# A recurrent attention layer with a gated feed-forward layer on one core: the order of every engine taken from a task graph with a list schedule, and deeper rings for the feed-forward weights

## The chip, the cores and the metric

The kernel runs on one core of a Trainium2 chip. TensorE (PE) multiplies matrices, VectorE (DVE) and ScalarE (ACT) do the element-wise work and copy results out of PSUM, GpSimd (POOL) does a few small things, and SyncE (SP) issues nearly all DMAs. Each engine works through its own queue in order; semaphores make one wait for another. The metric is the device time of one execution in microseconds. Before the change the median of three runs is 2511.51 us (2511.01 to 2513.72).

## What is computed

Two layers stand one behind the other, and the pair is applied twice. The first, A, is attention with a recurrent memory: the 2048 rows are cut into 64 segments of 32, and the output of a segment's first 8 rows is the memory of the next segment, so that the 64 segments must run one after the other. The second, B, is a gated feed-forward layer on each row.

```python
mem = mem0                                   # 8 rows of 512
for s in range(64):
    h = concat([mem, x[s*32:(s+1)*32]])      # 40 rows of 512
    q, k, v = h @ Wq, h @ Wk, h @ Wv         # 32 heads of 128
    p = softmax(mask(q @ k.T * scale))       # 40 x 40 in each head
    o = (p @ v) @ Wo                         # 40 rows of 512
    mem = o[:8]; out[s] = o[8:]
# B: out = (sigmoid(x @ w_gate) * (x @ w_up)) @ w_down, with 1792 hidden columns
x = x + A(layernorm(x));  x = x + B(layernorm(x))
x = x + A(layernorm(x));  x = x + B(layernorm(x))   # the same weights again
```

## The kernel before, in words

**Jobs and steps.** The two applications of A are two jobs, j = 0 and j = 1. Job 1 runs six segments behind job 0 (`LAG`), and one step works on one segment of each, so that the matmuls have 80 columns instead of 40. There are 70 steps: six with job 0 alone, 58 with both, six with job 1 alone. Blocks of four segments make 128 rows; layer B works on such a block ("an FFN block"): 16 blocks for each job, 32 in all.

**One step** (`emit_step`). The input of the step stands transposed in a slot of `hT`. For units of three heads PE computes q and k (L239) into one of three PSUM banks `pj`, ACT copies them to `qku`, PE multiplies them to scores in the bank `s_ps` (L255). Six heads make a group; for each group DVE adds the mask (L263), takes the maximum (L266), subtracts it (L267), ACT takes the exponential (L270), DVE sums (L272), inverts (L273) and multiplies (L277, once for each job) into `pb`. PE transposes `pb` into `pt_ps` (L289), and DVE copies it to `ptsb` (L99). Behind all groups come the values v (L325, `pj` again), the product p v (L336, bank `ot_ps`), its copy by ACT, and the product with Wo (L312, bank `wo_ps`, summed over all heads). At the end DVE copies the memory rows into the next slot of `hT` (L358): with that the next step can begin.

**One FFN block** (`task_post`). Behind the fourth step of a block PE transposes the attention output (L438), DVE adds the residual, a layernorm follows (DVE, one POOL instruction, ACT, a transpose on PE, L392), then seven pairs of hidden columns: 16 matmuls for gate and up (L460), a tanh on ACT, one DVE instruction that frees the bank, and last seven pieces of two matmuls with w_down (L496). All of this shares one PSUM bank, `misc`. The weights of B are loaded anew for each block, in pieces of 256 KB: `wg` and `wu` in rings of two, `wd` in a ring of two:

```python
self.gpool = ctx.enter_context(tc.tile_pool(name="gp", bufs=2))   # wg, wu
self.dpool = ctx.enter_context(tc.tile_pool(name="dp", bufs=2))   # wd
```

**What sets the order.** The code is written step by step; the FFN block of job 0 is emitted at once behind the fourth step, that of job 1 in four portions over four steps (`run`, `task_post`). The tile framework's scheduler then orders each engine's instructions by priorities that follow the order of emission; it may pull instructions ahead where a buffer is free.

Of the kernel before, what the change touches and what calls it, by code (L numbers as in the profile page):

```python
# [1 line left out]

# [19 lines left out]
LWP = LW  # L22
BLK = 4
EPS = 1e-5
PRIO_STEP = 1000000
# [5 lines left out]

class Kern:
    def __init__(self, ctx, tc, x_in, mem0, Wq, Wk, Wv, Wo, w_gate, w_up, w_down, out,
                 lag=6, ring=8, groups=None, npj=3, log=None):
        self.ctx, self.tc = ctx, tc
        self.nc = nc = tc.nc
        self.log = log
# [11 lines left out]
        self.LAG = lag  # L49
        self.R = ring  # L50
        assert ring > lag
        self.NSTEPS = self.NSEG + lag
        self.scale = float(DH) ** -0.5
        if groups is None:
            n6 = H // 6
            while n6 > 0 and (H - 6 * n6) % 4 != 0:
                n6 -= 1
            assert (H - 6 * n6) % 4 == 0
            sizes = [6] * n6 + [4] * ((H - 6 * n6) // 4)
            groups = []  # L60
            h = 0
            for sz in sizes:
                groups.append((h, sz))
                h += sz
            assert h == H
        self.groups = groups
        self.HG = max(sz for _, sz in groups)
        assert self.HG <= 6
# [4 lines left out]
        self.w_gate, self.w_up, self.w_down = w_gate, w_up, w_down  # L73
        self.npj = npj
        self.pj_i = 0
        self.ev_i = 0
        self.step_no = 0
        self.prio_idx = 0
        self._setup()

    def mark(self, tag, inst, g=-1):
        if self.log is not None:
            self.log.append((self.step_no, g, tag, inst.ins.name))
        return inst

    def set_prio(self, step, sub=0):
        base = int(max(step, 0) * PRIO_STEP + sub * (PRIO_STEP // 2))
        self.prio_idx += 1
        self.tc.cur_priority = base + self.prio_idx

    def evac(self, out, in_, prefer=None):
        nc = self.nc
        eng = prefer
        if eng is None:
            eng = "act" if (self.ev_i % 2 == 0) else "dve"
            self.ev_i += 1
        if eng == "act":
            return nc.scalar.copy(out=out, in_=in_)  # L98
        return nc.vector.tensor_copy(out=out, in_=in_)  # L99

    def next_pj(self):
        t_ = self.pj[self.pj_i % len(self.pj)]
        self.pj_i += 1
        return t_

    def _setup(self):
        self._setup_pools()
        self._load_first()
        self._setup_weights()

    def _load_first(self):
        self.load_mem0()
        for b in range(self.NBLK):
            if BLK * b - 4 < 0:
                self.pre1(b)

    def _setup_weights(self):
        nc = self.nc
        DC = self.DC
        wq_v = self.Wq.rearrange("(c p) h e -> p c (h e)", p=P)  # L120
        wk_v = self.Wk.rearrange("(c p) h e -> p c (h e)", p=P)
        wv_v = self.Wv.rearrange("(c p) h e -> p c (h e)", p=P)
        wo_v = self.Wo.rearrange("h e d -> e h d")
        loads = []
        for (h0, gsz) in self.groups:
            cs = slice(h0 * P, (h0 + gsz) * P)
            loads.append((self.wq[:, :, cs], wq_v[:, :, cs]))
            loads.append((self.wk[:, :, cs], wk_v[:, :, cs]))
        for (h0, gsz) in self.groups:
            cs = slice(h0 * P, (h0 + gsz) * P)  # L130
            loads.append((self.wv[:, :, cs], wv_v[:, :, cs]))
            loads.append((self.wo[:, h0:h0 + gsz, :], wo_v[:, h0:h0 + gsz, :]))
        for i, (dst, src) in enumerate(loads):
            nc.sync.dma_start(out=dst, in_=src)

    def _setup_pools(self):
# [3 lines left out]
        wpool = ctx.enter_context(tc.tile_pool(name="w", bufs=1))  # L140
        cpool = ctx.enter_context(tc.tile_pool(name="c", bufs=1))
        self.cpool = cpool
        self.wq = wpool.tile([P, DC, HE], BF16, name="wq_sb")
        self.wk = wpool.tile([P, DC, HE], BF16, name="wk_sb")
        self.wv = wpool.tile([P, DC, HE], BF16, name="wv_sb")
        self.wo = wpool.tile([P, H, D], BF16, name="wo_sb")
        self.ident = cpool.tile([P, P], BF16, name="ident")
# [5 lines left out]
        self.maskb = cpool.tile([P, L], F32, name="maskb")  # L153
# [4 lines left out]
        nc.sync.dma_start(out=self.maskb[JOFF:LW, :], in_=self.maskb[0:L, :])  # L158
        self.hT = cpool.tile([P, R, DC, LWP], BF16, name="hT_all")
        nc.vector.memset(self.hT[:], 0.0)  # L160
        self.qku = [cpool.tile([P, 3, 4, P], BF16, name=f"qku{i}") for i in range(3)]
        for t_ in self.qku:
            nc.gpsimd.memset(t_[:], 0.0)
        self.qku_i = 0
        self.vsb = [cpool.tile([P, HG * P], BF16, name=f"vsb{i}") for i in range(2)]
        for t_ in self.vsb:
            nc.gpsimd.memset(t_[:], 0.0)
# [26 lines left out]
    def emit_step(self, t):  # L194
# [64 lines left out]
        def emit_softmax(g, gsz):  # L259
# [25 lines left out]
            for hl in range(gsz):  # L285
                o_ap = pt_all[:, hl, cb:cb + ncol]
                if both:
                    o_ap = o_ap.rearrange("p (a b) -> p a b", a=2)
# [313 lines left out]
```

## Time and profile before

| what | before |
|---|---|
| timed runs | 2511.51 us median (2511.01 to 2513.72) |
| profiled execution, span | 2509.0 us |
| PE busy | 2186.8 us (87%) |
| DVE busy | 1322.3 us (53%) |
| ACT busy | 1217.0 us (49%) |
| read from HBM | 195.04 MB, 79 GB/s over the span |

The profile is of one execution, whose span lies 2.5 us below the median of the timed runs. PE's busy time is of matmuls whose ends are modelled and which overlap, so how much of the span PE really has nothing to start is read from the distance between the starts of matmuls, not from this share. A line in the timeline has the start, the time from the first start to the last end, the engine, the line of the kernel, what is written and read, and the count; in brackets is the idle time before it and what ended it.

### The profile page before, as it was taken

The numbers are of one execution on the slowest core, as the hardware profiler recorded it, in microseconds if no ns is written. First come the engines' busy times: TensorE is split into PE (matmuls) and PEld (weight loads), VectorE is DVE, ScalarE is ACT, GpSimd is POOL, SyncE is SP. The second block draws the span as 40 slices with busy tenths as digits, with TensorE's granted clock in tenths as the row PEclk, the third lists the DMA queues.
The fourth block names the chain that finished last, engine by engine and source line by source line (L and its number), as shares of the span: only waits on it lengthen the run. The fifth ranks groups of instructions, "written<-read, shape, count | busy, mean of one in ns | idle before, by whom it ended". The sixth has DMA issues, their size and how long they took to land.

```text
span 2509.0 us, 95297 instructions
## 1 busy us (share of the span) xinstructions
PE 2186.8 (87%) x42676; PEld 1839.6 (73%) x42676; DVE 1322.3 (53%) x3949; ACT 1217.0 (49%) x2829; POOL 52.2 (2%) x94
## 2 busy tenths in 40 slices
PE   5989898989888888898888889888888889988896
PEld 4877777777777777777777777777777777777673
DVE  4545555555555456455545655554564555455452
ACT  3545454545544454454545445454444545454452
POOL 1000000000000000000000000000000000000000
PEclk8999999999999999999999999999999999999997
DMA  9030204132231413213141421314132131413223
GB/s 303 5 91 10 85 19 134 50 108 60 63 94 47 134 35 112 71 48 106 50 134 34 121 63 56 97 51 134 34 111 71 44 107 50 130 35 102 81 62 97
DMA packets 314716, 203.28 MB, mean 81 GB/s; under 512 B 11706, under 2 KB 313794, under 8 KB 314306
## 3 DMA queue, kind: packets, MB, share of 16 engines
q1 hardware_dynamic: 313538, 195.10, 26.6%
q8 instruction: 333, 5.46, 0.9%
q0 software_dynamic: 768, 2.10, 0.2%
q14 instruction: 77, 0.63, 0.1%
HBM read 195.04 MB, written 2.10 MB: 79 GB/s over the span
## 4 chain that ended last, share of the span: by engine, by line
PE 35%; DVE 32%; DMA 19%; ACT 8%; issue 5%; POOL 1%; SPq 0%; ACTq 0%; POOLq 0%; DVEq 0%
PE wo_ps L312 8%; PE misc_ps L460 5%; DVE pb_98 L277 3%; DVE pb_97 L277 3%; PE pj_120 L325 3%; PE pj_121 L325 3%; PE misc_ps L496 3%; PE pj_122 L325 3%; DVE sm_104 L272 2%; PE pt_ps L289 2%; DVE mx_102 L266 2%; PE ot_ps L336 2%; DVE mx_101 L266 2%; DVE st_95 L263 2%; DVE st_96 L263 2%
## 5 line engine op out<-in xcount | busy, mean ns | idle before, releaser
L239 PEld LDWEIGHTS <-wk_sb 128*128 128x128 bf16 x8960 | 468.8, 99 | 9.6 <-issue 2.6
L239 PEld LDWEIGHTS <-wq_sb 128*128 128x128 bf16 x8960 | 457.2, 99 | 15.5 <-issue 8.6
L325 PEld LDWEIGHTS <-hT_all 128*104 128x104 bf16 x2800 | 316.6, 128 | 82.6 <-issue 1.2
L312 PEld LDWEIGHTS <-wo_sb 128*128 128x128 bf16 x8960 | 340.6, 99 | 20.2 <-issue 3.3
L239 PE MATMUL pj_121<-hT_all,wk_sb 128*128 128x80 bf16 (+1 forms) x2992 | 224.3, 198 | 2.5 <-issue 2.5
L239 PE MATMUL pj_122<-hT_all,wk_sb 128*128 128x80 bf16 (+1 forms) x2984 | 224.7, 199 | 0.0
L239 PE MATMUL pj_120<-hT_all,wk_sb 128*128 128x80 bf16 (+1 forms) x2984 | 223.8, 198 | 0.0
L239 PE MATMUL pj_122<-hT_all,wq_sb 128*128 128x80 bf16 (+1 forms) x2984 | 219.3, 198 | 2.0 <-DVE hT_all L363 1.3
L239 PE MATMUL pj_120<-hT_all,wq_sb 128*128 128x80 bf16 (+1 forms) x2984 | 218.8, 198 | 1.6 <-DVE hT_all L363 0.6
L239 PE MATMUL pj_121<-hT_all,wq_sb 128*128 128x80 bf16 (+1 forms) x2992 | 218.8, 198 | 1.7 <-DVE hT_all L358 0.6
L325 PE MATMUL pj_120<-wv_sb,hT_all 128*104 128x384 bf16 (+1 forms) x936 | 217.5, 342 | 0.0
L325 PE MATMUL pj_122<-wv_sb,hT_all 128*104 128x384 bf16 (+1 forms) x932 | 215.7, 341 | 0.0
L325 PE MATMUL pj_121<-wv_sb,hT_all 128*104 128x384 bf16 (+1 forms) x932 | 215.4, 342 | 0.0
L358 DVE CAST hT_all<-wo_ps 128x64 bf16<-128x64 f32 x57 | 12.8, 224 | 364.2 <-PE wo_ps L312 364.2
L312 PE MATMUL wo_ps<-otsb_113,wo_sb 128*128 128x80 bf16 (+1 forms) x4480 | 200.5, 198 | 1.4 <-ACT otsb_113 L98 1.4
L312 PE MATMUL wo_ps<-otsb_114,wo_sb 128*128 128x80 bf16 (+1 forms) x4480 | 187.0, 198 | 1.7 <-ACT otsb_114 L98 1.4
L263 DVE TENSOR_TENSOR st_95<-s_ps,maskb 104x240 f32<-104x240 f32 (+5 forms) x210 | 77.5, 369 | 179.1 <-PE s_ps L255 177.0
L277 DVE TENSOR_TENSOR pb_98<-st_96,rs_106 64x240 bf16<-64x240 f32 (+3 forms) x384 | 142.7, 372 | 4.7
L277 DVE TENSOR_TENSOR pb_97<-st_95,rs_105 64x240 bf16<-64x240 f32 (+3 forms) x384 | 142.5, 371 | 4.2
L270 ACT ACTIVATE st_95<-st_95 104x240 f32<-104x240 f32 (+5 forms) x210 | 79.7, 380 | 90.1 <-DVE st_95 L267 89.5
L98 ACT CAST otsb_114<-ot_ps 128x480 bf16<-128x480 f32 (+3 forms) x210 | 101.9, 485 | 31.6 <-PE ot_ps L336 31.3
L289 PE MATMUL pt_ps<-ident,pb_98 128*128 128x80 bf16 (+1 forms) x1120 | 74.3, 201 | 42.4 <-DVE pb_98 L277 41.5
(2396 smaller groups left out, 3996.9 us busy)
## 6 DMA issues: line engine op xcount, KB each, us to landing
wq_sb<-in_A_Wq_dram SPq DMA_DIRECT2D x4, 768.0 KB, 7.6
wk_sb<-in_A_Wk_dram SPq DMA_DIRECT2D x4, 768.0 KB, 9.5
wv_sb<-in_A_Wv_dram SPq DMA_DIRECT2D x4, 768.0 KB, 11.6
wo_sb<-in_A_Wo_dram SPq DMA_DIRECT2D x4, 768.0 KB, 10.9
wq_sb<-in_A_Wq_dram SPq DMA_DIRECT2D x2, 512.0 KB, 11.4
wk_sb<-in_A_Wk_dram SPq DMA_DIRECT2D x2, 512.0 KB, 11.6
wv_sb<-in_A_Wv_dram SPq DMA_DIRECT2D x2, 512.0 KB, 10.1
wo_sb<-in_A_Wo_dram SPq DMA_DIRECT2D x2, 512.0 KB, 9.0
```

The source lines that it names most:

```text
L98: return nc.scalar.copy(out=out, in_=in_)
L239: self.mark("qk_mm", nc.tensor.matmul(o_ap, lhsT=W[:, c, h * P:(h + 1) * P], rhs=mv(c), start=(c == 0), stop=(c == DC - 1)), g)
L263: self.mark("sm_mask", nc.vector.tensor_tensor(out=st[pr, hs], in0=s_all[pr, hs], in1=self.maskb[pr, :].unsqueeze(1).to_broadcast([npart, ...
L266: self.mark("sm_max", nc.vector.tensor_reduce(out=mx[pr, hs], in_=st[pr, hs], axis=AX.X, op=ALU.max), g)
L270: self.mark("sm_exp", nc.scalar.activation(out=st[pr, hs], in_=st[pr, hs], func=ACTF.Exp, scale=self.scale), g)
L272: self.mark("sm_sum", nc.vector.tensor_reduce(out=sm[pr, hs], in_=st[pr, hs], axis=AX.X, op=ALU.add), g)
L277: self.mark("sm_mul", nc.vector.tensor_tensor(out=pb[pj_, hs, JOFF * j:JOFF * j + L], in0=st[pj_, hs], in1=rs[pj_, hs].unsqueeze(2).to_bro ...
L289: self.mark("t_mm", nc.tensor.matmul(o_ap, lhsT=pb[:, hl, :], rhs=idn, start=True, stop=True), g)
L312: self.mark("wo_mm", nc.tensor.matmul(wo_ps[:, c * ncol:(c + 1) * ncol], lhsT=self.wo[:, h, c * P:(c + 1) * P], rhs=otsb[:, hl, 0:ncol], s ...
L325: self.mark("v_mm", nc.tensor.matmul(pv[0:LWP, 0:vun * P], lhsT=hT[:, c, :], rhs=self.wv[:, c, col0:col0 + vun * P], start=(c == 0), stop= ...
L460: nc.tensor.matmul(gu[:, 2 * i + k, :], lhsT=W[:, c, i * P:(i + 1) * P], rhs=xnT[:, c, :], start=(c == 0), stop=(c == DC - 1))
L496: nc.tensor.matmul(po, lhsT=hT[:, i, :], rhs=wd[:, k, :], start=(i == 0), stop=(i == FC - 1))
```

## The change

The attention's and the feed-forward layer's arithmetic stays as it is. What changes:

- **A task graph.** Each piece of work (one unit's 24 matmuls, one copy, one DVE instruction, one DMA) becomes a `Task` with an engine, an estimated duration and the keys of what it reads and writes. `Planner.plan` runs a list schedule over all tasks when the program is built: at each moment the engine that is free earliest takes, of its ready tasks, the one with the longest remaining chain (`tail`). The tasks are then emitted in the order of their planned starts, under `manual_schedule`, which keeps that order on each engine.
- **FFN pieces as tasks of their own**: half a pair (8 matmuls) and each w_down piece (2 matmuls) can stand anywhere between attention tasks. The order among users of the bank `misc` stays that of the code.
- **Rings**: `wg`, `wu` and `wd` of three buffers each instead of two; `hff` and `xnT` of one instead of two; `ptsb` of three instead of one for each group; `vsb` holds all heads.
- **Groups**: five groups of six heads and one of two (before: four of six, two of four); values in eight units of four heads (before: eight of three and two of four).
- **Engines**: the copies out of `pt_ps` and of the layernorm's transposes may go to ACT or DVE, as planned; the output DMA goes to SP's queue (before: POOL's). The last block no longer uses the `pj` banks.

```diff
+class Planner:
+    LAT = {"PE": 215.0, "DVE": 130.0, "ACT": 140.0, "POOL": 450.0, "SP": 2200.0}
...
+    def plan(self):
+        T = self.tasks
...
+        for tk in reversed(T):
+            m = 0.0
+            for s in tk.succ:
+                same = T[s].eng == tk.eng
+                m = max(m, T[s].tail + (0.0 if same else tk.lat))
+            tk.tail = m + tk.dur + tk.boost
...
+            while q and q[0][0] <= t:
+                _, i = heapq.heappop(q)
+                if T[i].on is None:
+                    heapq.heappush(h, (-T[i].tail, i))
...
+            tk = T[heapq.heappop(h)[1]]
+            tk.on, tk.start = e, t
+            free[e] = t + tk.dur
...
+        order.sort(key=lambda k: (k.start, k.idx))
+        return order
...
-        self.gpool = ctx.enter_context(tc.tile_pool(name="gp", bufs=2))
-        self.dpool = ctx.enter_context(tc.tile_pool(name="dp", bufs=2))
+        self.NG, self.ND = 3, 3
+        self.wg = [c.tile([P, DC, 2 * P], BF16, name=f"wg{i}") for i in range(self.NG)]
+        self.wu = [c.tile([P, DC, 2 * P], BF16, name=f"wu{i}") for i in range(self.NG)]
+        self.wd = [c.tile([P, 2, D], BF16, name=f"wd{i}") for i in range(self.ND)]
...
+            pl.add("SP", 870, lambda wg=wg, fs=fs: nc.sync.dma_start(out=wg[:], in_=self.wgv[:, :, fs]), w=[("wg", gi)])
...
+                pl.add("PE", 2 * DC * mm_ns(P), mm, r=[("xnT", ti), ("wg", gi), ("wu", gi)], w=["misc"])
...
+            pl.add("PE", 2 * mm_ns(512), dm, r=[("hff", hi, ip), ("wd", di)], w=["misc"])
...
+        order = self.pl.plan()
+        with self.tc.manual_schedule():
+            for tk in order:
+                got = tk.fn()
+                if isinstance(got, tuple):
+                    dst, src = got
+                    if tk.on == "ACT":
+                        nc.scalar.copy(out=dst, in_=src)
+                    else:
+                        nc.vector.tensor_copy(out=dst, in_=src)
```

Three places show what that does to the queues. The first is SP's queue around the w_down pieces of one FFN block (`wd`; `wg` and `wu` are gate and up pieces). Before, block 8 of job 0, its first two `wd` having been issued 26 rows earlier:

```order
L453 DMA wg_8_6_26555<-in_B_w_gate_dram 128x4x256
L454 DMA wu_8_6_26556<-in_B_w_up_dram 128x4x256
L453 DMA wg_6_5_27283<-in_B_w_gate_dram 128x4x256
L454 DMA wu_6_5_27284<-in_B_w_up_dram 128x4x256
L453 DMA wg_6_6_27306<-in_B_w_gate_dram 128x4x256
L454 DMA wu_6_6_27307<-in_B_w_up_dram 128x4x256
L493 DMA wd_8_2_26586<-in_B_w_down_dram 128x2x512
L493 DMA wd_8_3_26590<-in_B_w_down_dram 128x2x512
L493 DMA wd_8_4_26594<-in_B_w_down_dram 128x2x512
L493 DMA wd_8_5_26598<-in_B_w_down_dram 128x2x512
L493 DMA wd_8_6_26602<-in_B_w_down_dram 128x2x512
```

And now, at a w_down phase in the middle of the program (the number behind a name is the buffer's):

```order
L528 DMA wg_113<-in_B_w_gate_dram 128x4x256
L529 DMA wu_116<-in_B_w_up_dram 128x4x256
L528 DMA wg_111<-in_B_w_gate_dram 128x4x256
L529 DMA wu_114<-in_B_w_up_dram 128x4x256
L528 DMA wg_112<-in_B_w_gate_dram 128x4x256
L529 DMA wu_115<-in_B_w_up_dram 128x4x256
L551 DMA wd_118<-in_B_w_down_dram 128x2x512
L551 DMA wd_119<-in_B_w_down_dram 128x2x512
L551 DMA wd_117<-in_B_w_down_dram 128x2x512
L551 DMA wd_118<-in_B_w_down_dram 128x2x512
```

Two pieces can be on their way before, three now, and three gate and up pairs of the next block are now asked for ahead of the w_down pieces.

The second place is PE's queue just behind the first q and k unit of a step (`pj`: q, k or v of one unit; `hT`: the step's input). Before, an FFN pair follows and then the next q and k unit, and no v stands near:

```order
L239 LDWEIGHTS wk_sb
L239 MATMUL pj_121<-hT_all,wk_sb 128x80
L460 LDWEIGHTS wg_6_6_27306
L460 MATMUL misc_ps<-xnT_6_25621,wg_6_6_27306 128x128
...
L239 LDWEIGHTS wq_sb
L239 MATMUL pj_122<-hT_all,wq_sb 128x80
```

Now a unit of v, a w_down piece and another unit of v stand between the first unit of q and k and the second:

```order
L385 LDWEIGHTS wk_sb
L385 MATMUL pj_126<-hT_69,wk_sb 128x80
L451 LDWEIGHTS hT_69
L451 MATMUL pj_128<-wv_sb,hT_69 104x512
...
L556 LDWEIGHTS hff_108
L556 MATMUL misc_ps<-wd_119,hff_108 128x512
...
L451 LDWEIGHTS hT_69
L451 MATMUL pj_126<-wv_sb,hT_69 104x512
```

The values moved from the end of the step to its first half, between the units of q and k.

The third place is PE's queue at the seam between two steps. Before (the last Wo product, and what follows in the step at 1309 us of the profile), an FFN pair stands there:

```order
L312 LDWEIGHTS wo_sb
L312 MATMUL wo_ps<-otsb_114,wo_sb 128x80
L460 LDWEIGHTS wg_6_5_27283
L460 MATMUL misc_ps<-xnT_6_25621,wg_6_5_27283 128x128
...
L239 LDWEIGHTS wq_sb
L239 MATMUL pj_121<-hT_all,wq_sb 128x80
```

Now, at one of the seams, the next step's first unit follows at once (at others a w_down piece stands between):

```order
L535 LDWEIGHTS wu_115
L535 MATMUL misc_ps<-xnT_107,wu_115 128x128
L477 LDWEIGHTS wo_sb
L477 MATMUL wo_ps<-otsb_91,wo_sb 128x80
...
L385 LDWEIGHTS wq_sb
L385 MATMUL pj_127<-hT_70,wq_sb 128x80
```

The FFN pair moved to a place just ahead of the last Wo products, where PE would wait for their input.

More of the change, by code (lines that the diff above doesn't have):

```diff
@@ L139, in _setup_pools @@
         HE = H * P
[L140 to L147, printed above, removed]
+        c = ctx.enter_context(tc.tile_pool(name="c", bufs=1))
@@ new lines, in setup_tiles @@
+        self.wq = c.tile([P, DC, HE], BF16, name="wq_sb")
+        self.wk = c.tile([P, DC, HE], BF16, name="wk_sb")
+        self.wv = c.tile([P, DC, HE], BF16, name="wv_sb")
+        self.wo = c.tile([P, H, D], BF16, name="wo_sb")
+        self.ident = c.tile([P, P], BF16, name="ident")
+        self.maskb = c.tile([P, L], F32, name="maskb")
+        self.negh = c.tile([P, 1], F32, name="negh")
+        self.hT = [c.tile([P, DC, LW], BF16, name=f"hT{i}") for i in range(R)]
+        self.qku = [c.tile([P, 3, 4, P], BF16, name=f"qku{i}") for i in range(3)]
```

815 lines of the change are left out of this document (404 added, 411 removed).

## The prediction, made before the change was run

> **What bounds the kernel now.** The page comes first: PE is the busiest engine, yet the chain that ended last runs only to a third over PE.
>
> ```profile
> span 2509.0 us, 95297 instructions
> ...
> PE 35%; DVE 32%; DMA 19%; ACT 8%; issue 5%; POOL 1%; SPq 0%; ACTq 0%; POOLq 0%; DVEq 0%
> ```
>
> PE, DVE and DMAs take turns at holding up the work. How long a step is, the copy of the memory rows shows, which ends each two-job step but the last:
>
> ```profile
> L358 DVE CAST hT_all<-wo_ps x57: 223/224/225, 213.4 to 2253.5; 128x64 bf16<-128x64 f32 x57
> ...
>   PE wo_ps L312: 364.2, 57
> ```
>
> 56 distances in 2040.1 us are 36.43 us a step; and DVE stood idle 364.2/57 = 6.4 us before each copy, while PE did v, p v and Wo. Four neighbouring steps (length, then busy time and count on PE, PEld, DVE, ACT, POOL) are not alike:
>
> ```profile
> 1193.53:1226.64 33.11, 29.90 (x570) 24.62 (x569) 17.23 (x50) 15.87 (x36) 0.58 (x1) 1.00 0.20 62
> 1226.64:1259.46 32.82, 29.47 (x596) 25.41 (x594) 18.77 (x56) 17.56 (x40) 0.56 (x1) 1.00 0.12 35
> 1259.46:1309.00 49.54, 41.65 (x746) 34.64 (x744) 25.62 (x77) 22.32 (x50) 1.71 (x3) 1.00 0.51 148
> 1309.00:1339.48 30.48, 28.54 (x585) 24.79 (x583) 17.11 (x51) 16.60 (x38) 0.00 (x0) 1.00 0.13 37
> ```
>
> The third holds the whole FFN block of job 0 and takes 49.5 us. PE's timeline there gives the pace of each kind of matmul, by the distance of starts:
>
> ```profile
> 1272.44 0.39 PE L460 MATMUL misc_ps<-xnT_8_26398,wg_8_0_26417 128*128 128x128 bf16 x4
> 1272.66 0.39 PE L460 MATMUL misc_ps<-xnT_8_26398,wu_8_0_26418 128*128 128x128 bf16 x4
> ...
> 1273.33 0.38 PE L289 MATMUL pt_ps<-ident,pb_97 128*128 128x80 bf16 x6
> 1273.54 0.26 PE L255 MATMUL s_ps<-qku_86 128*128 128x40 bf16 x4
> 1273.65 0.30 PE L239 MATMUL pj_120<-hT_all,wq_sb 128*128 128x80 bf16 x4
> 1273.79 0.31 PE L239 MATMUL pj_120<-hT_all,wk_sb 128*128 128x80 bf16 x4
> ...
> 1289.57 0.59 PE L496 MATMUL misc_ps<-wd_8_0_26578,hff_8_26416 128*128 128x512 bf16 x2
> 1290.00 0.59 PE L496 MATMUL misc_ps<-wd_8_1_26582,hff_8_26416 128*128 128x512 bf16 x2
> ...
> 1301.84 1.04 PE L325 MATMUL pj_122<-wv_sb,hT_all 128*104 128x512 bf16 x4
> 1302.72 0.38 PE L336 MATMUL ot_ps<-ptsb_110,vsb_92 128*128 128x80 bf16 x6
> 1302.93 1.03 PE L312 MATMUL wo_ps<-otsb_113,wo_sb 128*128 128x80 bf16 x24
> 1303.80 0.82 PE L325 MATMUL pj_120<-wv_sb,hT_all 128*104 128x512 bf16 x3
> ```
>
> So four q or k matmuls take 0.14 us, four scores 0.11, six transposes or p v 0.21, four v of 512 columns 0.88, 24 of Wo 0.87, four gate or up matmuls 0.22, a w_down piece 0.43. By the program a two-job step has 256 q and k (9.1), 64 scores (1.7), 32 transposes and 32 p v (1.1 each), 32 v (7.0) and 128 Wo (4.6): 24.6 us. An FFN block has 112 gate and up matmuls (6.2), seven w_down pieces (3.0) and two or three transposes of 0.22: 9.8 us. Four steps with two blocks need 118.2 us of PE; they took 33.11 + 32.82 + 49.54 + 30.48 = 145.95. PE had nothing to start for 27.8 us, 7 a step. Two kinds of waits make that up:
>
> ```profile
>   DVE pb_98 L277: 41.5, 125
> ...
> 1264.45 0.40 PE L460 MATMUL misc_ps<-xnT_6_25621,wg_6_4_26369 128*128 128x128 bf16 x4 [1.36 <-DMA wg_6_4_26369<-in_B_w_gate_dram]
> ...
> 1293.91 0.59 PE L496 MATMUL misc_ps<-wd_8_2_26586,hff_8_26416 128*128 128x512 bf16 x2 [0.81 <-DMA wd_8_2_26586<-in_B_w_down_dram]
> ```
>
> PE waits for softmax at the transposes (41.5 us in all for one of the two `pb` buffers), and for FFN weights, whose next piece is asked for only when one of two buffers is free. The step at 1309 has two FFN pairs (24.6 + 1.8 = 26.4 us of PE) and still took 30.48: 4.1 us is what attention alone leaves idle; the rest, some 11 of the 27.8, is the FFN's.
>
> **FFN weights.** A piece lands 2.76 us after its issue where it is nearly alone, 4.70 where several are under way:
>
> ```profile
> 1200.68 0.37 SPq L493 DMA_DIRECT2D wd_5_6_24970<-in_B_w_down_dram  x1
> ...
> 1203.44 0.59 PE L496 MATMUL misc_ps<-wd_5_6_24970,hff_5_22620 128*128 128x512 bf16 x2 [0.54 <-DMA wd_5_6_24970<-in_B_w_down_dram]
> ...
> 1260.59 4.70 DMA wu_6_4_26370<-in_B_w_up_dram
> ```
>
> In the new order I add up, by these paces, the PE work between the last use of a ring slot and the next (with SP's queue in its order): a median of 11.8 us, and under 3.5 us for 38 of 672 pieces. With 2.76 us for every piece the shortfalls add up to 17 us, with 4.70 to 97: 0.2 and 1.4 us a step. I take 0.3, since most pieces now travel alone or in pairs. One output DMA and one load of x in four steps pass through the same SP queue, 0.37 us of issue each as above, under that slack. The FFN's 11 us are gone but for this.
>
> **Attention.** The change gives DVE the same instructions, with v now in the step's first half. DVE's round for one group of six heads:
>
> ```profile
> 1205.98 0.40 DVE L272 TENSOR_REDUCE sm_104<-st_96 104x6 f32<-104x240 f32 x1 [0.47 <-ACT st_96 L270]
> ...
> 1208.35 0.66 DVE L99 CAST ptsb_108<-pt_ps 128x480 bf16<-128x480 f32 x1
> 1208.92 0.39 DVE L272 TENSOR_REDUCE sm_103<-st_95 104x6 f32<-104x240 f32 x1
> ```
>
> 2.94 us a round, 0.57 of it the copy of `pt_ps`. 32 heads are 5.33 rounds, 15.7 us, and half of those copies now go to ACT. I walked one new step by hand through the queues, with an FFN load of 5.4 us, with these paces and for ACT and the way from PE to it:
>
> ```profile
> 1205.55 0.40 ACT L270 ACTIVATE st_96<-st_96 104x240 f32<-104x240 f32 x1
> ...
> 1206.46 0.31 PE L239 MATMUL pj_122<-hT_all,wk_sb 128*128 128x80 bf16 x4
> ...
> 1206.87 0.56 ACT L98 CAST qku_86<-pj_122 128x480 bf16<-128x480 f32 x1 [0.45 <-PE pj_122 L239]
> ```
>
> (0.27 us from the end of PE's 0.14 to ACT's start; 0.4 to 0.6 for its copies.) The first group's scores are complete 7.3 us into the step, behind four units of q and k, three of v, a w_down piece, four FFN transposes and the scores. Its transposes come only at 15.0, four us after softmax is done. From the fourth group DVE is level with PE: its list of 13 instructions between two products takes 5.3 us against 3.0 us of PE work. There the walk finds stalls of 0.64 (scores behind the mask instruction), 0.37 (an FFN half behind its DVE product), 0.17 (transposes), 0.10 (Wo behind its ACT copy). At the seam the last Wo, 0.27, the 0.22 copy and the next unit follow each other with nothing between: 0.5. Sum 1.8. In one step of four the FFN block's layernorm must also be through before the next step, for which I add 0.2 a step. With the weights' 0.3: **2.3 us idle a step**. Bounds: 0.8 (seam and weights alone) and 4.1 (as now, nothing covered; weights at 4.70 would give 3.4).
>
> **The sum**, against the span. 28 of the 32 blocks fall into the 58 two-job steps: 24.6 + 28 × 9.8/58 = 29.3 us of PE a step, plus 2.3: 31.6, rounded up to 31.7 for the loads' transposes. Against 36.43 over 56 steps that is 265 us less, 268 with the two at the ends. The ends:
>
> ```profile
> 0.00:184.77 184.77, 146.69 (x3274) 121.52 (x3275) 91.40 (x299) 81.87 (x223) 9.03 (x19) 0.94 0.43 135
> 99.33:120.79 21.46, 20.79 (x520) 17.63 (x520) 12.36 (x43) 12.28 (x35) 0.00 (x0) 1.00 0.02 4
> 2286.29:2464.00 177.71, 155.11 (x3476) 128.52 (x3474) 94.25 (x294) 89.77 (x236) 2.61 (x4) 0.98 0.29 82
> 2464.00:2509.00 45.00, 23.32 (x144) 13.86 (x143) 5.94 (x14) 4.08 (x9) 1.73 (x3) 0.60 0.42 126
> ...
> 2473.27 0.58 PE L438 MATMUL misc_ps<-ident,oxT_15_49613 128*128 128x128 bf16 x4 [0.78 <-DVE x_14_51622 L498]
> ...
> 2478.54 0.59 PE L460 MATMUL misc_ps<-xnT_15_51631,wg_15_0_51650 128*128 128x128 bf16 x4 [0.67 <-ACT xnT_15_51631 L98]
> ...
> 2486.76 0.64 PE L460 MATMUL pj_122<-xnT_15_51631,wg_15_3_51719 128*128 128x128 bf16 x4
> 2487.18 0.63 PE L460 MATMUL pj_122<-xnT_15_51631,wu_15_3_51720 128*128 128x128 bf16 x4
> ```
>
> The first six steps: the first waits for the same weights (54.5 us), five one-job steps at the quiet 21.46 and one block of 9.8 give 171.6 with it, 13 less. The last six: 6 × 21.46 + 2 × 9.8 = 148.4, 29 less. The tail is one block alone: 5.3 us from its first transpose to its first pair; seven pairs on a single bank at this clock (0.42 for four matmuls), 1.7 us and an estimate of 1.1 for the way through ACT (0.4) and DVE (0.4) and back, 2.8 each, 19.6; w_down with three in flight, where the seventh piece waits for the fourth and the fourth for the first: three pieces of 0.85 and two landings of 2.76, 8.1; the output about 3.5, an estimate from a landing and one DVE instruction. That is 36.5, 8.5 less than 45. In all 2509 − 268 − 13 − 29 − 8.5 = 2190.5, and 2.5 us more in the timed runs: **2193 us**. The granted clock of 0.60 in the tail bears on 6 us: at full clock a pair is 2.0. The Trainium skill (TensorE: Matmul & The Clock Gate, Part 1) has PE at full clock after some 3.4 us of sustained work, by which the tail would be 30 us; this trace disagrees, since pairs issued one behind the other from 2478.54 on still took 0.42 at 2487. The same page (Back-to-back issue gap) gives about 81 ns for each sustained 128-column matmul with its weight load; the 0.22 us for four here disagree. By it the 3584 gate and up matmuls would cost 93 us more and the time would be near 2286; with the row so plain I give that no chance.
>
> **Rivals.** (1) PE is kept fed: only seam and weights stay, 0.8 a step, 58 × 1.5 = 87 less: 2106. For it: softmax has four us of slack early in the step. Against: none late. 15%. (2) Attention's idle stays at 4.1 although v fills the first half, because a strict order makes PE wait for each late DVE result: 58 × 1.8 = 104 more: 2297. For it: DVE's last groups are level with PE. 14%. (3) Slower than before: FFN pieces now stand in front of attention work in PE's strict queue, and a late weight stops scores, transposes and Wo behind it, so DVE and ACT starve too. 672 pieces; from (2511 − 2193)/672 = 0.47 us of wait each the gain is gone; with the 0.81 seen for `wd_8_2` the time is 2193 + 544 = 2737. For it: SP's queue is strict as well. Against: 11.8 us of slack against 2.8 to 4.7. 5%. (4) No change, because the order on the chip would not be the planned one: the listings exclude that; 1% for any time within 0.2%, which is what these runs can tell.
>
> **Chances and range.** The forecast (2150 to 2270) has 62%, rivals (1) to (4) 15, 14, 5 and 1; 3% lie between (2) and the time before. Faster 94%, same 1%, slower 5%. The range 2105 to 2310 holds the forecast and the middle of (1) and (2).
>
> **What would show it.** Right: two-job steps of 31 to 33 us without the long fourth one; DVE's wait before the memory copy far under 6.4 us; few DMA waits before FFN matmuls; PE's remaining waits behind DVE in the last third of a step. Wrong: FFN matmuls released by DMA again, steps of 34 us or more, or a tail longer than 37 us.

## The result

The changed kernel takes **2197.28 us** (median of four runs, 2195.44 to 2199.14) against 2512.61 us for the kernel before (2511.01 to 2516.22): a ratio of **0.8746**, 95% interval 0.8733 to 0.876. It is 315 us faster; 2193 us was forecast.

### The profile page after: what moved, and what is told of

Same layout as the page of the kernel before. It is cut to its first block, busy times and chain, and to the rows that moved or that the text cites. A ratio compares the mean times of both kernels' runs of the same rounds, so it can differ in the third digit from the quotient of the medians.

```text
span 2196.4 us, 93329 instructions
## 1 busy us (share of the span) xinstructions
PE 2056.8 (94%) x42116; PEld 1742.8 (79%) x42116; DVE 1270.8 (58%) x3743; ACT 1299.0 (59%) x2919; POOL 43.5 (2%) x77
## 4 chain that ended last, share of the span: by engine, by line
PE 62%; DVE 29%; issue 3%; ACT 3%; DMA 2%; POOL 0%; DVEq 0%; POOLq 0%; ACTq 0%
PE pj L385 22%; PE pj L451 16%; PE misc_ps L535 7%; PE wo_ps L477 7%; DVE pb L426 7%; DVE st L410 4%; DVE mx L413 3%; DVE st L415 3%; DVE sm L420 3%; PE misc_ps L556 3%; PE s_ps L403 3%; DVE ptsb L601 2%; DMA wd<-in_B_w_down_dram 2%; PE ot_ps L461 2%; PE pt_ps L436 2%
## 5 line engine op out<-in xcount | busy, mean ns | idle before, releaser
L385 PE MATMUL pj<-hT,wq_sb 128*128 128x80 bf16 (+1 forms) x8960 | 626.4, 198 | 16.1 <-DVE hT L488 13.6
L385 PE MATMUL pj<-hT,wk_sb 128*128 128x80 bf16 (+1 forms) x8960 | 627.6, 198 | 0.0
L451 PE MATMUL pj<-wv_sb,hT 128*104 128x512 bf16 x2240 | 568.3, 384 | 1.8 <-ACT vsb L599 1.6
L385 PEld LDWEIGHTS <-wq_sb 128*128 128x128 bf16 x8960 | 465.2, 99 | 59.6 <-issue 21.7
L599 ACT CAST qku<-pj 128x480 bf16<-128x480 f32 (+3 forms) x770 | 389.4, 514 | 144.4 <-PE pj L385 103.9
L599 ACT CAST vsb<-pj 104x512 bf16<-104x512 f32 (+2 forms) x560 | 326.1, 585 | 229.4 <-PE pj L451 223.4
L477 PE MATMUL wo_ps<-otsb,wo_sb 128*128 128x80 bf16 (+1 forms) x8960 | 389.3, 198 | 4.6 <-ACT otsb L599 4.2
L451 PEld LDWEIGHTS <-hT 128*104 128x104 bf16 x2240 | 253.3, 128 | 128.1 <-issue 5.1
L410 DVE TENSOR_TENSOR st<-s_ps,maskb 104x240 f32<-104x240 f32 (+5 forms) x420 | 158.0, 376 | 296.7 <-PE s_ps L403 290.0
L426 DVE TENSOR_TENSOR pb<-st,rs 64x240 bf16<-64x240 f32 (+3 forms) x768 | 287.9, 375 | 26.7 <-DVE rs L422 0.5
L599 ACT CAST otsb<-ot_ps 128x480 bf16<-128x480 f32 (+3 forms) x420 | 204.4, 487 | 66.6 <-PE ot_ps L461 60.4
L403 PE MATMUL s_ps<-qku 128*128 128x40 bf16 x4096 | 201.6, 180 | 24.5 <-DVE st L410 21.7
L544 DVE SCALAR_TENSOR_TENSOR hff<-th,misc_ps 128x256 bf16<-128x256 f32 x224 | 93.4, 417 | 210.6 <-ACT th L542 208.9
L436 PE MATMUL pt_ps<-ident,pb 128*128 128x80 bf16 (+1 forms) x2240 | 145.4, 198 | 32.8 <-DVE pb L426 27.8
L413 DVE TENSOR_REDUCE mx<-st 104x6 f32<-104x240 f32 (+5 forms) x420 | 156.9, 374 | 13.5
```

The costliest lines, as they stand in the source:

```text
L385: nc.tensor.matmul(o_ap, lhsT=W[:, c, h * P:(h + 1) * P], rhs=mv(c), start=(c == 0), stop=(c == DC - 1))
L403: nc.tensor.matmul(s_all[:, uh - h0 + i, :], lhsT=qku[:, i, j, :], rhs=qku[:, i, 2 + j, JOFF * j:JOFF * j + L], start=(idx == 0), stop=(id ...
L410: pl.add("DVE", dve_ns(n, True), lambda gsz=gsz, hs=hs, st=st: nc.vector.tensor_tensor(out=st[pr, hs], in0=s_all[pr, hs], in1=self.maskb[p ...
L413: pl.add("DVE", dve_ns(n), lambda hs=hs, st=st, mx=mx: nc.vector.tensor_reduce(out=mx[pr, hs], in_=st[pr, hs], axis=AX.X, op=ALU.max), r=[ ...
L426: pl.add("DVE", dve_ns(n), lambda gsz=gsz, hs=hs, st=st, rs=rs, pb=pb, pj_=pj_, npj_=npj_, j=j: nc.vector.tensor_tensor(out=pb[pj_, hs, JO ...
L436: nc.tensor.matmul(o_ap, lhsT=pb[:, hl, :], rhs=idn, start=True, stop=True)
```

## The profile after

The page of the changed kernel: the span, and the engines of the chain that ended last.

```profile
span 2196.4 us, 93329 instructions
...
PE 62%; DVE 29%; issue 3%; ACT 3%; DMA 2%; POOL 0%; DVEq 0%; POOLq 0%; ACTq 0%
```

PE's share of the chain has gone from 35 to 62%, the DMAs' from 19 to 2%; DVE's is almost what it was. The copy of the memory rows (L358 before, L488 now) with its first and last start, and what ended DVE's idle time before it:

```profile
L488 DVE CAST hT<-wo_ps x57: 223/225/226, 202.7 to 1979.6; 128x64 bf16<-128x64 f32 x57
...
  PE wo_ps L477: 112.9, 56
```

56 distances in 1776.9 us are 31.73 us a step (36.43 before), and DVE is idle 2.0 us before each copy instead of 6.4. The stretches of the program and four neighbouring steps (length, then busy time and count on PE, PEld, DVE, ACT, POOL; granted clock, DMA share, GB/s):

```profile
0.00:174.98 174.98, 139.33 (x3226) 113.04 (x3227) 92.22 (x287) 87.95 (x237) 11.12 (x18) 0.94 0.47 147
174.98:2011.49 1836.51, 1756.90 (x35412) 1500.85 (x35412) 1083.96 (x3175) 1116.61 (x2436) 30.20 (x55) 1.00 0.31 88
2011.49:2160.07 148.58, 140.09 (x3345) 114.71 (x3344) 89.39 (x268) 90.37 (x237) 1.65 (x3) 1.00 0.27 78
...
1024.26:1057.40 33.14, 31.30 (x598) 25.64 (x598) 20.31 (x60) 18.78 (x43) 0.55 (x1) 1.00 0.37 106
1057.40:1086.49 29.09, 27.57 (x584) 24.02 (x584) 17.97 (x56) 19.22 (x41) 1.10 (x2) 1.00 0.06 18
1086.49:1119.63 33.14, 31.92 (x634) 27.22 (x634) 17.35 (x50) 19.70 (x44) 0.00 (x0) 1.00 0.44 131
1119.63:1151.32 31.69, 31.00 (x636) 27.14 (x636) 19.69 (x57) 19.84 (x43) 0.55 (x1) 1.00 0.37 103
```

The long step of 49.5 us is gone; the four take 127.1 us instead of 145.95 for the same 118.2 us of PE work, so 8.9 us idle instead of 27.8. The tail, from the last block's first transpose on, in its three parts:

```profile
2160.07:2164.91 4.84, 0.79 (x8) 0.50 (x9) 1.61 (x5) 1.40 (x2) 0.55 (x1) 0.96 0.36 114
2164.91:2184.46 19.55, 13.05 (x112) 11.92 (x112) 2.95 (x7) 2.69 (x7) 0.00 (x0) 0.50 0.38 108
2184.46:2196.40 11.94, 6.61 (x14) 1.78 (x13) 0.69 (x1) 0.00 (x0) 0.00 (x0) 0.50 0.31 99
```

What PE waited for, in us in total, times, and the longest:

```profile
PE pt_ps L436 <- DVE pb L426: 27.8, 41, 2.9
PE s_ps L403 <- DVE st L410: 21.7, 32, 1.1
PE misc_ps L324 <- ACT xn L318: 19.3, 17, 3.4
PE pj L385 <- DVE hT L488: 13.6, 43, 0.3
...
PE misc_ps L556 <- DMA wd<-in_B_w_down_dram: 8.6, 10, 2.2
```

That view leaves out waits that fall to a weight load. By the distances of matmul starts, less the pace of each kind, PE idles 133.4 us in the 58 two-job steps, 2.30 us a step (before: 402.9, 6.95). Per step it stands before scores 0.55, before the transposes of `pb` 0.44, before q and k 0.36, before a layernorm's transposes 0.32, before w_down 0.16, before Wo 0.14, p v 0.13, v 0.11, gate and up 0.09.

## The experiments

### Was it the third buffer?

First the changed kernel with rings of two:

```diff
-        self.NG, self.ND = 3, 3
+        self.NG, self.ND = 2, 2
```

> The changed kernel with two buffers instead of three for each of wg, wu and wd; the planner orders it anew. Theory A (the order brings the FFN's gain: pieces lie far enough apart for two buffers as well): with 11.8 us of median slack for three buffers, two leave about half, 5 to 6 us, still above a landing of 2.76 to 4.70; only the pieces that stand close together wait. 0.2 to 0.7 us a two-job step more than now: 2205 to 2240. Theory B (the third buffer brings it): the 11 us in four steps come back, 58/4 x 11 = 160: 2340 or more, with DMA named before most gate and up matmuls.

Measured: 2194.94 us (ratio 0.8746, 0.8733 to 0.8759), the same as with three. Theory A stands, without even the small loss that it expected. PE's wait for w_down is no longer than with three buffers (8.6 us):

```profile
PE misc_ps L556 <- DMA wd<-in_B_w_down_dram: 6.3, 6, 1.9
```

Then the other way round, the kernel before with rings of three:

```diff
-        self.gpool = ctx.enter_context(tc.tile_pool(name="gp", bufs=2))
-        self.dpool = ctx.enter_context(tc.tile_pool(name="dp", bufs=2))
+        self.gpool = ctx.enter_context(tc.tile_pool(name="gp", bufs=3))
+        self.dpool = ctx.enter_context(tc.tile_pool(name="dp", bufs=3))
```

> The kernel before with three buffers instead of two for wg, wu and wd, its order left to the scheduler as it was. Theory A (order): seven pieces of a kind in a burst outrun a third buffer too; one more pair (1.8 us of PE) and one w_down piece (0.43) are loaded ahead in each of 32 blocks, at most some 2 to 3 us a block: 2415 to 2480. Theory B (depth): most of the 11 us in four steps goes, 160 us: 2340 to 2380.

Measured: 2438.62 us (0.9721, 0.9701 to 0.9741), 71 us less, as theory A has it. The waits of that kernel:

```profile
PE pt_ps L289 <- DVE pb L277: 83.4, 251, 1.6
PE misc_ps L496 <- DMA wd<-in_B_w_down_dram: 49.1, 65, 2.0
PE misc_ps L392 <- ACT xn_f L389: 30.0, 30, 3.4
```

A burst of w_down pieces outruns three buffers too (49.1 us, against 8.6 in the new order). So depth is worth 71 us where pieces stand in bursts, and nothing measurable in the changed kernel.

### What is attention's share, what the FFN's?

Both kernels without the FFN's weights, pairs and w_down, each in one execution. The core of the edit in the changed kernel:

```diff
-        for jp in range(FC // 2):
...
-        for ip in range(FC // 2):
...
-        pl.add("DVE", dve_ns(D, True), lambda: nc.vector.scalar_tensor_tensor(out=xo[:], in0=po, scalar=0.5, in1=xa[:], op0=ALU.mult, op1=ALU.add),
-               r=["misc", ("xa", xi)], w=[ok])
+        pl.add("DVE", dve_ns(D, True), lambda: nc.vector.tensor_copy(out=xo[:], in_=xa[:]),
+               r=[("xa", xi)], w=[ok])
```

> The kernel before without the FFN's weights, gate and up, tanh, product and w_down (its layernorms and residual stay); an FFN block then passes its input on. This prices attention alone in the old order. Theory A (the prediction's split, read from one step at 1309): 24.6 us of PE and 4.1 idle, 28.7 a two-job step. Theory B (the step at 1309 was not typical; by the distances of matmul starts 190 of 403 us of idle in the two-job steps stand before attention's matmuls, 3.3 a step): 27.9. In all about 58 x 28.7 or 27.9, with 173 for the first six steps, 129 for the last six and 8 behind them: 1975 or 1928.

> The changed kernel without the same FFN work. Theory A (the planned order by itself, with v in the first half, leaves 1.8 to 2.0 us of idle a step, as the prediction has it): 26.6 a two-job step, 165 + 58 x 26.6 + 129 + 8 = 1845. Theory B (attention's waits are as long as before, 4 us, and what the change does is to put FFN pieces into them): 28.6 or more, 1960.

The spans and the copies of the memory rows, first of the kernel before without its FFN, then of the changed one:

```profile
span 2037.4 us, 85532 instructions
...
L358 DVE CAST hT_all<-wo_ps x57: 223/225/226, 193.3 to 1859.5; 128x64 bf16<-128x64 f32 x57
```

```profile
span 1934.1 us, 83564 instructions
...
L488 DVE CAST hT<-wo_ps x57: 211/223/226, 194.9 to 1761.5; 128x64 bf16<-128x64 f32 x57
```

29.75 us a step before, 27.97 after. In the kernel before, the time lies above both theories: steps without layernorm work do take 28.7, which is the 4.1 of idle that the prediction read, but those with it take 30.5 to 31.2, so that the mean idle is about 4.8 (29.75 less 24.6 and 0.3 of layernorm transposes). In the changed kernel it lies between the theories, nearer to B. Without the FFN the change is worth 2037.4 - 1934.1 = **103 us**. That is not the order alone: the groups, the units of v and the copies out of `pt_ps` that went to ACT changed with it, and these copies are worth 39 us in the whole kernel (as the run with all of them on DVE shows further down). The FFN adds 2509.0 - 2037.4 = 471.6 us before and 2196.4 - 1934.1 = 262.3 after: **209 us** less. Its left-out matmuls are 32 x 9.2 = 294 us of PE. Before, it cost 177 us more than that; now it costs 32 less, although some 30 us of its last block stand alone behind the last step (36.9 us from the start of the last Wo to the end with the FFN, 6.3 without): its other pieces lie in attention's waits.

### Spread over the steps, or only cut into pieces?

```diff
-                pl.add("PE", 2 * DC * mm_ns(P), mm, r=[("xnT", ti), ("wg", gi), ("wu", gi)], w=["misc"])
+                pl.add("PE", 2 * DC * mm_ns(P), mm, r=[("xnT", ti), ("wg", gi), ("wu", gi)], w=["misc"], boost=3e4)
...
-            pl.add("PE", 2 * mm_ns(512), dm, r=[("hff", hi, ip), ("wd", di)], w=["misc"])
+            pl.add("PE", 2 * mm_ns(512), dm, r=[("hff", hi, ip), ("wd", di)], w=["misc"], boost=3e4)
```

> The changed kernel, but every FFN matmul task is put ahead of attention tasks that are ready at the same time (30 us added to its remaining chain in the planner), so that a block runs in a denser stretch instead of filling gaps over 40 us. Theory A (the gain is the filling of attention's waits with FFN pieces): the filler is spent early, steps without FFN pieces idle as the step at 1309 did (4.1 instead of 2.3 in about one step of two), 58 x 0.5 x 1.8 = 50 more, and weights wait more: 2230 to 2290. Theory B (what counts is only that pieces stand singly between attention work and that the order is fixed): 2190 to 2210.

Measured: 2228.97 us (0.8882, 0.8868 to 0.8896), 32 us slower than the change, just below theory A's range. Two neighbouring steps show its mechanism:

```profile
976.92:1005.02 28.10, 25.82 (x544) 21.97 (x544) 16.06 (x46) 16.75 (x36) 0.00 (x0) 1.00 0.01 3
1005.02:1041.16 36.14, 34.83 (x675) 29.89 (x678) 21.57 (x62) 21.43 (x47) 1.09 (x2) 1.00 0.55 159
```

Steps now alternate: one with hardly a load (3 GB/s) at 28.1 us, as long as attention alone, and one with the FFN's load at 36.1. The filler is missing in the first.

### Where does attention's idle sit?

```diff
-        self.ptsb = [c.tile([P, HG, 2 * L], BF16, name=f"ptsb{i}") for i in range(3)]
+        self.ptsb = [c.tile([P, HG, 2 * L], BF16, name=f"ptsb{i}") for i in range(6)]
...
+        kept = []
...
-            pi = self.nxt("ptsb", 3)
+            pi = self.nxt("ptsb", 6)
...
+            kept.append((pi, ptsb))
+
+        for g, (h0, gsz, us) in enumerate(self.groups):
+            hs = slice(0, gsz)
+            pi, ptsb = kept[g]
             for n0 in range(0, H, 4):
```

> The changed kernel with v, p v and Wo recorded behind all groups of a step, as the kernel before had them, with six ptsb buffers instead of three; the planner still orders it. Theory A (the prediction's place of the idle is right: DVE is level with PE in the last third, because v is used up in the first half): v late gives PE 7 us of work that waits for no DVE, and the stalls of 0.64, 0.17 and 0.10 a step go: 58 x 0.9 = 50 less, about 2145 to 2160. Theory B (v in the first half is what brought attention's idle from 4.1 down to 2): it comes back, 58 x 1.8 to 2.3 = 104 to 133 more, about 2300 to 2330.

Measured: 2144.45 us (0.8545, 0.8532 to 0.8558): 53 us faster than the change, theory A. The waits of this kernel, the first line for the end of the step (L493 is the copy of the memory rows here), the others for the bank `misc` and for softmax:

```profile
PE pj L386 <- DVE hT L493: 14.9, 46, 0.7
PE misc_ps L540 <- DVE hff L549: 14.8, 38, 0.9
PE pt_ps L437 <- DVE pb L427: 13.3, 7, 2.9
...
PE s_ps L404 <- DVE st L411: 3.3, 17, 0.2
```

The wait for scores falls from 21.7 us to 3.3, that for `pb` from 27.8 to 13.3. What moved, the traces show for the 50 two-job steps in the middle, as a share of the step: the median start of a v matmul goes from 0.40 to 0.57 and that of the scores from 0.43 to 0.31, while p v (0.71 and 0.73) and Wo (0.84 and 0.86) stay. So the early place of v, which the change brought with it, cost time. Even in the change v is not all early: 45% of its matmuls start in the second half of a step. Whether late v helps as work that waits for no DVE, or because q, k and the scores come earlier and DVE can begin earlier, is not separated; nor are the six `ptsb` buffers, which belong to the edit.

The second test of the same place puts all copies of `pt_ps` on DVE:

```diff
-            pl.add(("ACT", "DVE"), dve_ns(gsz * ncol, True), lambda hs=hs, ptsb=ptsb: (ptsb[:, hs, 0:ncol], pt_all[:, hs, 0:ncol]), r=["pt_ps"], w=[("ptsb", pi)])
+            pl.add("DVE", dve_ns(gsz * ncol, True), lambda hs=hs, ptsb=ptsb: (ptsb[:, hs, 0:ncol], pt_all[:, hs, 0:ncol]), r=["pt_ps"], w=[("ptsb", pi)])
```

> The changed kernel with the copy of pt_ps to ptsb always on DVE, where now the planner gives 241 of 420 to ACT. Theory A (DVE is level with PE in the last third of a step, so its work there is on the path): of 5.33 copies a step about 3 go back, 3 x 0.57 = 1.7 us more on DVE; half of that shows: 58 x 0.9 = 50 more, 2240 to 2260. Theory B (DVE is busy only 58% and hides it): 2190 to 2205.

Measured: 2235.86 us (0.8907, 0.8888 to 0.8926), 39 us more: theory A's direction, a little under its size. Work on DVE is on the path although DVE is busy only 58% of the span. (The trace of the change has 250 of the 420 copies on ACT, not 241.)

### Is DVE late because the plan has it wrong?

A stretch of DVE's timeline in the changed kernel (start, duration):

```profile
1106.93 0.41 DVE L415 TENSOR_TENSOR st<-st,mx 104x240 f32<-104x240 f32 x1
1107.25 0.41 DVE L544 SCALAR_TENSOR_TENSOR hff<-th,misc_ps 128x256 bf16<-128x256 f32 x1
1107.58 0.40 DVE L410 TENSOR_TENSOR st<-s_ps,maskb 104x240 f32<-104x240 f32 x1
1108.02 0.40 DVE L413 TENSOR_REDUCE mx<-st 104x6 f32<-104x240 f32 x1
1108.45 0.41 DVE L415 TENSOR_TENSOR st<-st,mx 104x240 f32<-104x240 f32 x1
```

The FFN product (L544) starts 0.32 us after the subtraction, with which it has nothing to do; the maximum (L413) starts 0.44 us after the masked scores (L410), which it needs. The planner knows only the shorter distance.

```diff
-    return n / 0.96 + (42.0 if psum else 70.0)
+    return n / 0.96 + 75.0
...
-    LAT = {"PE": 215.0, "DVE": 130.0, "ACT": 140.0, "POOL": 450.0, "SP": 2200.0}
+    LAT = {"PE": 215.0, "DVE": 138.0, "ACT": 150.0, "POOL": 300.0, "SP": 2200.0}
+    SAME = {"PE": 0.0, "DVE": 115.0, "ACT": 115.0, "POOL": 0.0, "SP": 0.0}
...
-                m = max(m, T[s].tail + (0.0 if same else tk.lat))
+                m = max(m, T[s].tail + (self.SAME[tk.eng[0]] if same else tk.lat))
...
-                n.ready = max(n.ready, t + tk.dur + (0.0 if same else tk.lat))
+                n.ready = max(n.ready, t + tk.dur + (self.SAME[e] if same else tk.lat))
```

> The changed kernel with the planner's costs set to what the profile shows: a DVE or ACT instruction that needs the one just before it on its engine starts 0.43 us after it (240 elements), where the planner has 0.29 to 0.32; so 115 ns are added between dependent tasks of one engine, 75 ns fixed cost for every DVE instruction, and the ways from DVE, ACT and POOL to others are 138, 150 and 300 ns. Nothing else changes. Theory A (PE waits behind DVE because the plan has DVE's results too early by 0.12 us an instruction, some 0.8 us a group): most of the 73 us of idle before scores, transposes, p v and Wo in the two-job steps goes, and some of the 25 in the first six: 2100 to 2140. Theory B (DVE is level with PE at the end of a step, whatever the plan knows): 2185 to 2205.

Measured: **2090.13 us** (0.832, 0.8301 to 0.8339), 107 us faster than the change and under theory A's range. DVE's timeline in this kernel:

```profile
1109.87 0.40 DVE L421 TENSOR_REDUCE sm<-st 104x6 f32<-104x240 f32 x1 [0.47 <-ACT st L419]
1110.19 0.40 DVE L411 TENSOR_TENSOR st<-s_ps,maskb 104x240 f32<-104x240 f32 x1
1110.50 0.18 DVE L423 RECIPROCAL rs<-sm 104x6 f32<-104x6 f32 x1
1110.62 0.40 DVE L414 TENSOR_REDUCE mx<-st 104x6 f32<-104x240 f32 x1
1110.94 0.39 DVE L427 TENSOR_TENSOR pb<-st,rs 64x240 bf16<-64x240 f32 x1
```

The plan now lays two groups' chains into each other, so that each of these starts behind one it does not need: 0.31 to 0.32 us behind those of 240 elements, 0.12 behind the short reciprocal. By the distances of starts 39.6 us of idle are left in the two-job steps, 0.7 a step. The edit sets several numbers at once; which of them does how much was not separated. The planner also gives DVE less: 125 of the 420 copies out of `pt_ps` instead of 170. At the price of the run above (39 us for 250 copies) these 45 would be 7 us, an estimate, so most of the 107 us is not that.

> Both edits together: v recorded last and the planner's costs as the profile shows them. Theory A (two remedies for one stall, DVE late in the last third): less than the sum, about 2080 to 2120, near the better of the two. Theory B (they act in different places): the gains add, 2144 less what the costs alone bring.

Measured: 2082.52 us (0.8292, 0.827 to 0.8314). The two together give 115 us, where 53 and 107 would add up to 160: theory A, two remedies for one stall. With the measured costs only 39.6 us of idle were left in the two-job steps, so the full 53 could hardly have come on top.

### What do the weights still cost?

```diff
-            pl.add("SP", 870, lambda wg=wg, fs=fs: nc.sync.dma_start(out=wg[:], in_=self.wgv[:, :, fs]), w=[("wg", gi)])
+            if self.cnt["wg"] <= self.NG:
+                pl.add("SP", 870, lambda wg=wg, fs=fs: nc.sync.dma_start(out=wg[:], in_=self.wgv[:, :, fs]), w=[("wg", gi)])
```

and the same for `wu` and `wd`.

> The changed kernel, with the FFN weights loaded only into the three buffers of each ring at the start and never again (the later blocks use what lies there, so the FFN's values are not the reference's). It prices all that the loads still cost. Theory A (the prediction's term: 0.3 us a two-job step, as w_down matmuls still wait 8.6 us and the weight loads before FFN matmuls some 10 to 25 more): 15 to 30 us less, 2168 to 2183. Theory B (two buffers were as good as three, so nothing is left to gain): 2190 to 2200. Theory C (the transfers also slow the engines beside them): under 2150.

Measured: 2166.42 us (0.8625, 0.8606 to 0.8644): 31 us less, just beyond theory A's 15 to 30. The planner also orders anew here, so some of it may be a luckier order: the wait for scores, which is for no weight, falls from 21.7 to 7.0 us.

The rings of two once more, now with the measured planner costs:

> The changed kernel with the measured planner costs (2090.1) and two buffers instead of three for wg, wu and wd. In the changed order two buffers cost nothing; with these costs PE idles only 40 us in the two-job steps, so there is less idle time for a late weight to hide in. Theory A (the depth still does not matter, the order does): 2085 to 2097. Theory B (the depth was free only because attention's own waits covered it; a w_down matmul in a ring of two can wait for a landing of 2.76 once in a while, and the planner then moves pieces apart): 20 to 30 us more, 2108 to 2122.

Measured: 2108.38 us (0.8394, 0.8375 to 0.8412), 18 us more than with three buffers, just inside theory B. The waits of this kernel:

```profile
PE pj L386 <- DVE hT L489: 22.6, 43, 1.0
PE pt_ps L437 <- DVE pb L427: 19.6, 23, 2.9
...
PE misc_ps L557 <- DMA wd<-in_B_w_down_dram: 5.2, 5, 1.7
```

With three buffers they are 14.4, 13.9 and 4.6 us. So PE hardly waits longer for weights; it waits longer behind DVE, in the other order that the planner lays for two buffers. That the third buffer is worth 18 us here is measured. That attention's waits covered for it in the change is argued only, and an unluckier order would look the same.

### The tail, and the fastest kernel

Beside v last and the measured costs:

```diff
-        self.NG, self.ND = 3, 3
+        self.NG, self.ND = 3, 4
...
-            gu = self.misc[:, :].rearrange("p (a n) -> p a n", a=4)
+            bank, bk = self.misc, "misc"
+            if j == 1 and b == self.NBLK - 1 and jp % 4:
+                bank, bk = self.pj[jp % 4 - 1], ("pj", jp % 4 - 1)
+            gu = bank[:, :].rearrange("p (a n) -> p a n", a=4)
```

> The kernel with v last and the measured planner costs (2082.5), and beside it: the last FFN block's seven pairs take turns in misc and the three pj banks, and wd has four buffers. Theory A (the tail's pair is 2.8 us because one bank holds 1.7 us of matmuls and 1.1 of ACT and DVE in series): 7 x 1.1 = 7.6 less, and the w_down pieces behind it, with four in flight and two landings less to wait for, some 2 less: 2070 to 2076. Theory B (the tail's clock, 0.6, and not the bank sets its pace, and four w_down buffers do nothing): 2078 to 2086. Theory C (w_down's place in the order holds up other pieces in the two-job steps too): 2045 to 2060.

Measured: **2064.16 us** (0.8219, 0.8203 to 0.8234), the fastest of all: 18 us less than without these edits, between theories A and C. From the last Wo's start to the end it takes 26.5 us instead of 37.0, some 10 of the 18, which is A's size; the rest comes from the two-job steps, and since the two edits were made together, which of them brings that stays open. The tail's parts:

```profile
2037.79:2042.85 5.06, 1.00 (x8) 0.67 (x9) 1.61 (x5) 1.40 (x2) 0.55 (x1) 0.75 0.36 99
2042.85:2047.07 4.22, 4.22 (x40) 4.21 (x40) 0.61 (x2) 0.77 (x2) 0.00 (x0) 0.50 0.13 35
2047.07:2063.76 16.69, 8.60 (x88) 5.25 (x86) 3.02 (x7) 1.92 (x5) 0.00 (x0) 1.00 0.58 173
```

With four banks the pairs follow each other without the 1.1 us between them, as A has it. That the clock then rises was not in A: PE, at first without gaps, gets its full clock after 4.2 us, which it never does in the tail of the changed kernel. From there on PE waits for weights, 4.6 us in seven waits of up to 1.08.

## Why the prediction was right, and where not

**The sum.** Each term came out near its forecast in the profiled execution (the tail's last two are divided at 2193.01, where DVE takes the last sum out of `misc`):

| term | forecast | measured |
|---|---|---|
| first six steps | 171.6 | 174.98 |
| a two-job step | 31.7 | 1836.51 / 58 = 31.66 |
| last six steps | 148.4 | 148.58 |
| tail: to the first pair | 5.3 | 4.84 |
| seven pairs | 19.6 | 19.55 |
| w_down | 8.1 | 8.55 |
| output | 3.5 | 3.39 |

The forecast terms of this table add up to 2195.1, not to the 2190.5 that the prediction made of them. The slip is its "268 with the two at the ends": the first and the last two-job step took 28.7 and 32.8 us before, so that 31.7 saves nothing there, and 263 would have been right. Added rightly, the terms give 2197.6 for the timed runs, against 2197.28 measured.

That close a match is partly luck. The first six steps are off by 3.4: the first ends at 57.0, not 54.5, and one-job steps take 22.1, not 21.46. The last six hit because two errors cancel: six steps of 22.1 are 132.8, and their two FFN blocks add only 15.8 us, not 19.6, since pieces lie in attention's waits.

**The idle of a step** was 2.3 us as forecast, its parts less so. Right: scores behind the mask instruction (0.64 forecast, 0.55), Wo (0.10, 0.14). Mis-sized: the transposes behind `pb` (0.17, measured 0.44), the FFN half behind its DVE product (0.37, 0.09), the seam (0.5, 0.36), the layernorm (0.2, 0.32). The weights' 0.3 are 0.16 as direct waits, and 0.5 by the run without the loads (31 us over 58 steps and the ends). One step walked by hand gave the size and the place, not the shares.

**The split of the gain.** The prediction had FFN waits at 11 of the 27.8 us and attention at 4.1 a step. Without the FFN a step took 29.75 and 27.97 us, so 1.8 us a step are attention's own gain (the forecast: 4.1 to 1.8, 2.3) and the other 2.9 of the 4.7 the FFN's (forecast: 11/4 less 0.3, some 2.5). The sum was right partly because these two errors cancel. Part of what the prediction put down to attention's order is FFN pieces standing in attention's waits.

**The rings.** The slack of 11.8 us was taken for rings of three, and the depth for a part of the gain. With two buffers nothing is lost (6.3 us of waits for w_down), so the new order ends these waits without the third buffer.

**Rivals.** (1), PE kept fed, was refused because nothing covers the last third. For this order that is so; but DVE's amount of work does not force it: the same kernel, planned with measured DVE distances and with 45 copies fewer on DVE, idles 0.7 us a step and takes 2090, near that rival's 2106. (2), attention's idle of 4.1, did not come: 2.3. Its remark "although v fills the first half" had the sign wrong, since the kernel with v late is 53 us faster. (3), pieces that block PE's queue, is refuted: 8.6 us of waits for w_down in all. (4) is refuted by the steps.

**What was to be seen** was seen: steps of 27.7 to 35.5, nearly all between 29 and 34, none long every fourth time; DVE's wait before the memory copy 2.0; few DMA waits. The place of the waits behind DVE is only half right. Of the 31.7 us before scores, the largest item, 30 stand between 50 and 60% of the step; the transposes (22 of 25.6 us), p v and Wo do wait in the last third. In the step at 1086.49 the first two stand at 60 and 73% of it:

```profile
1106.51 0.46 PE L403 MATMUL s_ps<-qku 128*128 128x40 bf16 x12 [0.31 <-DVE st L410]
...
1110.75 0.39 PE L436 MATMUL pt_ps<-ident,pb 128*128 128x80 bf16 x6 [0.60 <-DVE pb L426]
```

## What to carry to other kernels

Before a list schedule is trusted, hold its costs against the trace, and look above all for the distance of two instructions on one engine where the second needs the first: here a planner with measured costs, of which this distance of 0.12 us was one, was worth 107 us, a third of what the whole rewrite brought. Whether a deeper ring helps depends on the order around it: the same third buffer gave 71, 0 and 18 us in three orders. To find what work is worth as a filler, leave it out and compare the time that it adds with its own engine time.

## What the runs showed of the hardware that was not expected

**The clock of the tail.** In the change PE is busy 13.05 of 19.55 us during the seven pairs (1.7 us of matmuls, then a gap, 2.79 each), and the granted clock stays at 0.50 throughout. In the fastest kernel 4.22 us without a gap raise it to 1.00, where it stays for the last 16.69 us although PE is busy for only 8.60 of them. The prediction held against the Trainium skill (TensorE: Matmul & The Clock Gate, Part 1: full clock after some 3.4 us of sustained work) that pairs in the old tail still ran at half pace after 9 us; but only the first 3.4 us of them were without a gap. Then, in the timeline of the kernel before:

```profile
2483.02 0.61 PE L460 MATMUL pj_121<-xnT_15_51631,wg_15_2_51696 128*128 128x128 bf16 x4 [0.90 <-DMA wg_15_2_51696<-in_B_w_gate_dram]
2484.17 0.61 PE L460 MATMUL pj_121<-xnT_15_51631,wu_15_2_51697 128*128 128x128 bf16 x4 [0.54 <-DMA wu_15_2_51697<-in_B_w_up_dram]
```

The runs agree with the rule once "sustained" is taken to mean without such gaps. Shorter ones do not always matter: in the same trace the granted clock goes from 0.50 to 1.00 at 2493.7 us, although by the distances of starts gaps of 0.2 and 0.4 us stand in the 3.4 us before. Where the limit lies was not tried.

**DVE's distance between instructions** differs where the second needs the first: 0.44 us against 0.32 for 240 elements, both with 0.40 to 0.41 of duration. Need is not the only cause. The two multiplications into `pb` of one group (L426), of which neither reads what the other writes, start 0.41 us apart (median of 305 pairs in the changed kernel). What holds the second back was not tested.
